# One Fourier row half folded in a new order, small copies moved between engines, and weight loads tied to a later step

## The chip, the cores and the metric

The kernel runs on one core of a Trainium2 chip. A core has a matrix engine (TensorE, in the profile PE; its weight loads are the row PEld), a vector engine (VectorE, DVE), an activation engine (ScalarE, ACT), a general engine (GpSimd, POOL) and a sync engine (SP) that here only issues transfers. Each engine works through its own list of instructions strictly in order. Transfers issued by POOL go into one queue (q0 in the profile), those issued by SP into another (q1), and both are carried by the same 16 DMA engines. The metric is the time of the program on the device in microseconds (us); lower is better.

## What is computed

The reference has two parts. The first is chunked attention over 4 batches of 8 heads, 768 rows and 64 columns: each chunk of 32 rows looks at 8 memory keys and at the rows from 16 before to 8 after it. The second takes the attention output x (4 x 768 x 512) and mixes it:

```python
X = np.fft.fft(x, axis=1)
X = np.fft.fft(X, axis=2)
mixed = np.real(X).astype(np.float32)
u = x + mixed
mu = np.mean(u, axis=-1, keepdims=True)
var = np.mean((u - mu) ** 2, axis=-1, keepdims=True)
un = (u - mu) / np.sqrt(var + 1e-06)
ch = np.maximum(un @ w_ch1, 0.0) @ w_ch2
return (u + ch).astype(np.float32)
```

## The kernel before

The heads are taken in 16 pairs, four to a batch (`HP` = 4). A pair n goes through `attention(n)` (L867): its q and k are loaded by POOL, its v by SP; q and k are transposed on PE and copied out of the transpose bank (`e_qT`, `e_kT`); the memory keys are copied into the key tile (`e_mkT`, L404); then come scores, exponentials on ACT, the products with v on PE, and a normalisation on DVE (`e_norm`) that writes the pair's columns of `xsb`. The 768 rows stand as six tiles of 128 rows; "half g" means three of them, and `t_norm[n, g]` is the task that finishes half g of pair n.

A batch whose four pairs are done is Fourier transformed. For batch 0 this is `first_fourier` (L997), which works in half rows so that it can begin before the last pair is done. It uses symmetry: with `par` 0 and 1 (even and odd columns of the result) and `ab` 0 and 1 (cosine and sine part), four folded tiles of 128 columns are made from the 512 columns of x. In `before` one fold takes three steps on DVE: `g_zy` (L591) adds or subtracts columns 0-127 and 256-383 (the two pairs that are done first); `g_ff(..., last=0)` (L598) adds or subtracts columns 129-255 read backwards, and sets the small column 0 of the fold by a copy or a zero; `g_ff(..., last=1)` adds or subtracts columns 385-511 read backwards, and for (par, ab) = (1, 1) sets column 0 by a subtraction. Columns 128-255 belong to the pair done third (n = 2) and columns 384-511 to the one done last (n = 3), so only the last step waits for the last pair.

After a fold ACT rounds it to 16 bits (`g_hi`, L627), DVE makes the rest that rounding left (`g_lo`, L631), and PE multiplies both with tables of cosines and sines (`g_rows`, L656): 12 matmuls for each of the eight (half, par, ab), besides two groups of one-row matmuls (`g_row`, L644) for the middle column, which POOL prepares (`g_mid`, L636). Then the row result is split again (`e_up` on ACT, `e_rest` and `e_dn` on DVE), the column transform is done on PE (`e_columns`, L669, tile `pm`), the sum, mean and variance on DVE, the centred rows on ACT (`e_un`), their transposes on PE and copies on DVE (`e_unT`). Only then can the two matrix products of batch 0 run: `e_ch1` (L734, tile `ph`) with the first weights, `e_ch2` (tile `pc`) with the second. From there on PE is to be kept full with these products, which are marked as fillers, while attention and Fourier steps of the later batches go on beside them.

What runs when is decided in Python before anything is emitted. `Plan` (L37) holds tasks with an engine, an assumed cost, the tasks they come after, and the buffers that they take and give. It goes through an imagined time and gives each free engine the first task, by rank, that is ready; the rank is the order of creation where none is given. The chosen order is then fixed on each engine. So an assumed cost that changes can change the order everywhere. Where PE has nothing ready before the first fold is done, dummy matmuls are placed (`e_fill`, L825, tile `idle`). `behind=t` holds a task back until task t has been placed; it adds no wait on the chip, but puts the instruction later into its engine's list.

POOL's list around the change is: the q and k loads of pairs 4 and 5, `g_mid(0)`, four loads of the first weights `w1` (L988, 512 KB each as stored, cast from 32 to 16 bits), `g_mid(1)` among them, the loads of pair 6, four loads of the second weights `w2` (L993), the loads of pair 7 and so on. The q and k loads use three buffers each, those of v four. Loads of pair 6 are placed behind the last `w1` load, and `w2` behind the loads of pair 6 (`t_ck`). The `w1` loads are placed behind `t_norm[3, 1]`. A list `t_mark` collects the task of the last fold step of (par, ab, half) = (0, 0, 1); nothing uses it in `before`.

## Time and profile before

| | |
|---|---|
| median of 7 runs | 287.92 us (286.25 to 293.1) |
| the profiled execution | 286.05 us, its span 284.3 us |
| granted TensorE clock, mean | 0.998 |
| PE, DVE, ACT, POOL busy | 268.1, 166.0, 158.9, 58.0 us |
| PE busy from 65.4 to 218.0 us | 151.98 of 152.60 us |

The span is the time from the first to the last instruction; 1.75 us of the profiled execution lie outside it. PE counts as busy with dummy matmuls too, and matmuls overlap, so a busy PE says that it was fed, not that it did needed work. A row of the timeline gives start, length, engine, line, operation, the tiles written and read, and in brackets how long the engine had waited and for what.

### The profile page before, as it was taken

To read this page: it belongs to the slowest core of one execution; us is meant where nothing else is said; L and a number is where in the kernel's file an instruction comes from. 1 tells how busy PE (TensorE), PEld (TensorE's weight loads), DVE (VectorE), ACT (ScalarE), POOL (GpSimd) and SP (SyncE) were. 2 spreads that over 40 slices of the span, in tenths; PEclk is the share of its full clock that TensorE was granted. 3 is DMA by queue.
4 is the path that set the end of the run, shared out by engine and by line. 5 is a ranking of instruction groups with operands and counts; after the bars stand their busy time and mean duration, and the time that the engine had idled before them with its cause. 6 is when DMAs were issued, how large, how long until landed. Compare 5 with 4: busy or idle time off the path is not lost.

```text
span 284.3 us, 7145 instructions
## 1 busy us (share of the span) xinstructions
PE 268.1 (94%) x2943; PEld 171.0 (60%) x2943; DVE 166.0 (58%) x359; ACT 158.9 (56%) x286; POOL 58.0 (20%) x106
## 2 busy tenths in 40 slices
PE   0599998999999999999999999999999999999994
PEld 0466797766575666755756655556754645545644
DVE  7968998972077953899874990887396012012012
ACT  6887448597755578447735468047634722712700
POOL 8844643231210272621010020101002000000000
PEclk9999999999999999999999999999999999999999
DMA  6999999999999999999986462397024434004204
GB/s 106 201 179 159 192 203 201 198 196 191 185 213 237 137 221 177 169 174 212 218 112 155 125 138 48 114 148 220 2 41 107 113 73 112 2 37 111 39 37 111
DMA packets 116112, 39.92 MB, mean 140 GB/s; under 512 B 104560, under 2 KB 111472, under 8 KB 116080
## 3 DMA queue, kind: packets, MB, share of 16 engines
q1 hardware_dynamic: 93888, 23.54, 45.5%
q0 software_dynamic: 21472, 15.21, 33.4%
q10 hardware_dynamic: 720, 0.72, 0.8%
q8 instruction: 23, 0.38, 0.5%
q14 instruction: 9, 0.07, 0.1%
HBM read 37.36 MB, written 13.37 MB: 178 GB/s over the span
## 4 chain that ended last, share of the span: by engine, by line
PE 77%; DMA 13%; POOL 6%; issue 1%; DVE 1%; ACT 0%; POOLq 0%; DVEq 0%
PE pc L752 29%; PE ph L737 28%; DMA qs<-in_q_dram 9%; PE ps L527 5%; DMA w_sb<-in_moe_w_ch_dram 4%; PE xa L455 4%; PE xo L455 3%; PE pm L677 3%; PE sc L431 2%; PE idle L828 1%; PE trq L375 1%; DMA out_dram<-osb 1%; PE trk L375 1%; PE pm L578 1%; POOL qs L347 1%
## 5 line engine op out<-in xcount | busy, mean ns | idle before, releaser
L737 PE MATMUL ph<-unT,w_sb 128*128 128x384 f16 x512 | 88.5, 326 | 0.6 <-ACT hT L745 0.6
L745 ACT ACTIVATE hT<-ph 128x384 f16<-128x384 f32 x128 | 62.0, 493 | 47.2 <-PE ph L737 45.8
L752 PE MATMUL pc<-w_sb,hT 128*128 128x512 f16 x368 | 83.8, 379 | 0.0
L737 PEld LDWEIGHTS <-w_sb 128*128 128x128 f16 x512 | 48.5, 98 | 32.8 <-issue 1.8
L752 PEld LDWEIGHTS <-hT 128*128 128x128 f16 x368 | 34.8, 98 | 39.3 <-issue 0.4
L777 DVE SCALAR_TENSOR_TENSOR osb<-pc,rstd,xsb 128x512 f32<-128x512 f32 x23 | 17.3, 750 | 60.3 <-PE pc L752 58.8
L439 ACT ACTIVATE e<-sc,mbias 128x384 f32<-128x384 f32 x64 | 33.6, 578 | 11.1 <-PE sc L431 10.9
L697 ACT ACTIVATE un<-xsb,mu_s 128x512 f16<-128x512 f32 x24 | 17.1, 722 | 19.2 <-DVE mu_s L692 19.2
L691 DVE BATCH_NORM_STATS2 st<-xsb 128x6 f32<-128x512 f32 x24 | 16.6, 692 | 0.7
L539 ACT CAST up<-ps 128x386 f16<-128x386 f32 x16 | 9.7, 604 | 11.9 <-PE ps L527 10.5
L512 ACT CAST hi<-ff 128x768 f16<-128x768 f32 x12 | 9.9, 830 | 9.8 <-DVE ff L504 9.8
L455 PEld LDWEIGHTS xa<-va,e 128*64 128x64 f32 x384 | 12.6, 138 | 4.4 <-issue 3.4
L455 PE MATMUL xa<-va,e 128*64 128x65 f32 x384 | 14.9, 227 | 0.0
L544 DVE TENSOR_TENSOR up<-ps,up 128x386 f16<-128x386 f32 x16 | 9.6, 597 | 8.5 <-ACT up L539 8.5
L455 PE MATMUL xo<-va,e 128*64 128x65 f32 x384 | 14.1, 223 | 0.0
L431 PE MATMUL sc<-qT,kTb 64*128 64x64 bf16 x384 | 11.5, 194 | 2.7 <-ACT e L439 1.9
L431 PEld LDWEIGHTS <-kTb 64*128 64x128 bf16 x384 | 8.0, 96 | 10.1 <-issue 7.1
L517 DVE TENSOR_TENSOR lo<-ff,hi 128x768 f16<-128x768 f32 x12 | 11.3, 952 | 4.5 <-ACT hi L512 4.4
L683 DVE TENSOR_TENSOR xsb<-pm,xsb 128x512 f32<-128x512 f32 x15 | 10.1, 675 | 4.8 <-PE pm L677 4.7
L465 DVE RECIPROCAL zs<-xa 128x6 f32<-128x6 f32 x16 | 3.0, 188 | 17.0 <-PE xa L455 16.9
L455 PEld LDWEIGHTS xo<-va,e 128*64 128x64 f32 x384 | 12.6, 138 | 0.4 <-ACT e L439 0.3
L487 DVE TENSOR_TENSOR zy<-xsb 128x768 f32<-128x768 f32 x12 | 11.4, 954 | 0.1
(149 smaller groups left out, 357.4 us busy)
## 6 DMA issues: line engine op xcount, KB each, us to landing
va<-in_v_dram SPq DMA_DIRECT2D x32, 220.0 KB
w_sb<-in_moe_w_ch_dram POOLq DMA_DIRECT2D x8, 512.0 KB, 15.0
out_dram<-osb SPq DMA_DIRECT2D x12, 256.0 KB
qs<-in_q_dram POOLq DMA_DIRECT2D x12, 192.0 KB, 6.4
ks<-in_k_dram POOLq DMA_DIRECT2D x12, 192.0 KB, 6.7
x_rows<-xsb POOLq DMA_DIRECT2D x3, 768.0 KB, 5.3
xr<-x_back POOLq DMA_DIRECT2D x3, 768.0 KB, 5.3
out_rows<-osb SPq DMA_DIRECT2D x9, 256.0 KB
```

The source lines that it names most:

```text
L431: nc.tensor.matmul(sc[:, hh, t6, :], kT[r0:r0 + 64, t, :], qT[r0:r0 + 64, ts(t, 64)], start=True, stop=True, tile_position=(r0, 0))
L439: nc.scalar.activation(e1[:, :, :, ts(half, 32)], sc[:, :, 0:6, ts(half, 32)], AFT.Exp, bias=mbias[:, half:half + 1], scale=1.0 / math.sqr ...
L455: nc.tensor.matmul(xa[64 * half:64 * half + 64, st, hh, 0:65], e1[:, hh, t6, :], v1[:, hh, 6 * g + t6, 0:65], start=True, stop=True)
L487: nc.vector.tensor_tensor(zy_of[b, par][:, :, c0:c0 + P], xb[:, :, c0:c0 + P], xb[:, :, HD + c0:HD + c0 + P], ALU.add if par == 0 else ALU ...
L517: nc.vector.tensor_tensor(lo[:, ab].rearrange(fl), ff_of[b, par][:, ab].rearrange(fl), hi[:, ab].rearrange(fl), ALU.subtract)
L527: nc.tensor.matmul(out_[:, sp, :], part[:, ab, sp * 3 + st, c0:c1], tab[:, sp, st, :], start=(st == 0 and i == 0), stop=(st == 2 and i == 1))
L691: nc.vector.bn_stats(st6, xs[b][:, kt, :])
L697: nc.scalar.activation(un, xs[b][:, kt, :], AFT.Identity, bias=mu_of[b][:, kt, 0:1], scale=-1.0)
L737: nc.tensor.matmul(ph[:, 0:384], w1_sb[:, dt, ts(ht, P)], unT_of[b][:, dt, sh * 384:(sh + 1) * 384], start=(dt == 0), stop=(dt == NDT - 1))
L745: nc.scalar.activation(hT_of[b, sh][:, ht, :], ph[:, 0:384], AFT.Relu, bias=0.0, scale=-1.0)
L752: nc.tensor.matmul(pc_of[b, sh, stl], hT_of[b, sh][:, ht, ts(stl, P)], w2_sb[:, ht, :], start=(ht == 0), stop=(ht == NHT - 1))
L777: nc.vector.scalar_tensor_tensor(osb, pc, rstd_of[b][:, st:st + 1], xs[b][:, st, :], ALU.mult, ALU.add)
```

## The change

In half 1 of the first Fourier transform, columns 128-255 and 384-511 (of the pairs n = 2 and n = 3) are now first added or subtracted in reading order (`g_w`, twice, once for each par), into the unused half of the `zy` tile. The fold is then one step from two sums (`g_both`, four times), where it had been two steps (eight times). Half 0 keeps its two steps. The small column 0 of each fold becomes an instruction of its own (`g_col`): seven of the eight are done on ACT and one, (1, 1) of half 0, on POOL at rank 20.1, just behind `g_mid(0)`. `g_hi` waits for its column as well. The memory keys of pair 4 (n == `HP`) are copied by ACT in place of DVE. Assumed costs change: 0.5 for the first fold steps that had 0.62, 0.25 for the memory keys that had 0.2. The `w1` loads are placed behind the fold of (0, 0, 1), now a `g_both`, and no longer behind the last normalisation.

```diff
--- before.py
+++ after.py
@@ -403,7 +403,7 @@
 
     def e_mkT(n):
         b, pr = seq[n]
-        nc.vector.tensor_copy(
+        (nc.scalar.copy if n == HP else nc.vector.tensor_copy)(
             kTb[n % NKT][:, :, MEM0:MEM0 + NMEM],
             mkT[:, b * HP + pr, :].unsqueeze(1).to_broadcast([P, NT, NMEM]))
 
@@ -603,16 +603,34 @@
         plus = ab == par
         if last:
             plus = plus == (par == 0)
-        if not last:
-            if ab == 0:
-                nc.vector.tensor_copy(ff[:, :, 0], zy[:, :, 0])
-            elif par == 0:
-                nc.vector.memset(ff[:, :, 0:1], 0.0)
-        elif (par, ab) == (1, 1):
-            nc.vector.tensor_tensor(ff[:, :, 0], xb[:, :, P], xb[:, :, HD + P], ALU.subtract)
         nc.vector.tensor_tensor(ff[:, :, 1:P], (ff if last else zy)[:, :, 1:P],
                                 rev_ap(xb, 2 * P - 1 + HD * last, P - 1, [[DM, 3]]),
                                 ALU.add if plus else ALU.subtract)
+
+    def g_w(par):
+        xb, sl = xs[0][:, 3:6], slice(0, 3)
+        nc.vector.tensor_tensor(zy_of[0, par][:, sl], xb[:, :, P:2 * P], xb[:, :, HD + P:HD + 2 * P],
+                                ALU.add if par == 0 else ALU.subtract)
+
+    def g_col(par, ab, g):
+        zy = zy_of[0, par]
+        ff = ff_of[0, par][:, ab, 3 * g:3 * g + 3]
+        if ab == 0:
+            nc.scalar.copy(ff[:, :, 0], zy[:, 3 * g:3 * g + 3, 0])
+        elif par == 0:
+            nc.scalar.copy(ff[:, :, 0], zero[:, 0:1].to_broadcast([P, 3]))
+        elif g == 1:
+            nc.scalar.copy(ff[:, :, 0], zy[:, 0:3, 0])
+        else:
+            xb = xs[0][:, 0:3]
+            nc.gpsimd.tensor_tensor(ff[:, :, 0], xb[:, :, P], xb[:, :, HD + P], ALU.subtract)
+
+    def g_both(par, ab):
+        zy = zy_of[0, par]
+        ff = ff_of[0, par][:, ab, 3:6]
+        nc.vector.tensor_tensor(ff[:, :, 1:P], zy[:, 3:6, 1:P],
+                                rev_ap(zy, P - 1, P - 1, [[P, 3]]),
+                                ALU.add if ab == par else ALU.subtract)
 
     def g_hl(par, which):
         if (par, 0) not in g_of:
@@ -882,7 +900,7 @@
                 nc.gpsimd.tensor_copy(gate[64:65], va[n % NV][64:65, 1, NT - 1, 0:1])
 
             t_gate = add("POOL", 0.1, e_gate, [lv])
-        mk = t_mk[n] = add("DVE", 0.2, lambda: e_mkT(n), [t_mkT, t_kTz[n % NKT], t_mk.get(n - 1)],
+        mk = t_mk[n] = add("ACT" if n == HP else "DVE", 0.25, lambda: e_mkT(n), [t_mkT, t_kTz[n % NKT], t_mk.get(n - 1)],
                            take=("kTb",), behind=t_norm.get((HP - 1, 1)) if n in (HP, HP + 1) else None)
         if b >= TURNED:
             eq = add("SP", 1.2, lambda: e_flip_q(n), [lq], take=("qT",), give=("qs",),
@@ -987,7 +1005,7 @@
         if n == HP + 1:
             t_w1.extend(add("POOL", 0.7, lambda dt=dt: nc.gpsimd.dma_start(
                 w1_sb[:, dt, :], moe_w_ch1[ts(dt, P), :]), moved=2.4, grain=0.32, late=2.0,
-                behind=t_norm[HP - 1, 1], rank=t_ck[n]["rank"] + 0.1) for dt in range(NDT))
+                behind=t_mark[0], rank=t_ck[n]["rank"] + 0.1) for dt in range(NDT))
             t_ck[n] = t_w1[-1]
         else:
             t_w2.extend(add("POOL", 0.7, lambda g=g: nc.gpsimd.dma_start(
@@ -1001,25 +1019,45 @@
                 zy = add("DVE", 0.5, lambda par=par, g=g: g_zy(par, g),
                          [t_norm[0, g], t_norm[1, g], t_sines],
                          take=("unT",) if g == 0 else ())
+                if g == 1:
+                    w_ = add("DVE", 0.52, lambda par=par: g_w(par), [zy, t_norm[3, 1], pre[par, 1, 0]])
+                    for ab in range(2):
+                        col = add("ACT", 0.25, lambda par=par, ab=ab: g_col(par, ab, 1),
+                                  [w_ if par else zy, pre[par, ab, 0]])
+                        pre[par, ab, 1] = [w_, zy, col]
+                    continue
                 for ab in range(2):
-                    pre[par, ab, g] = add("DVE", (0.62 if ab == 0 else 0.5),
+                    pre[par, ab, g] = add("DVE", 0.5,
                                           lambda par=par, ab=ab, g=g: g_ff(par, ab, g, 0),
                                           [zy, t_norm[2, g]],
                                           take=("fold",) if (ab, g) == (0, 0) else (),
                                           give=("unT",) if (ab, g) == (1, 1) else ())
             t_mid[g] = add("POOL", 0.9, lambda g=g: g_mid(g), [t_norm[2, g], t_norm[3, g]],
                            rank=20)
+            if g == 0:
+                for par in range(2):
+                    for ab in range(2):
+                        pool = (par, ab) == (1, 1)
+                        pre[par, ab, 2] = add("POOL" if pool else "ACT", 0.4 if pool else 0.25,
+                                              lambda par=par, ab=ab: g_col(par, ab, 0),
+                                              [pre[par, 0, 0], t_norm[3, 0] if pool else None],
+                                              rank=20.1 if pool else None)
             t_row[g] = add("PE", 1.2, lambda g=g: g_row(g), [t_mid[g], t_neg, t_row.get(0), t_dz],
                            take=("acc",) if g == 0 else ())
             for par in range(2):
                 for ab in range(2):
                     end = (ab, g) == (1, 1)
-                    ff = add("DVE", 0.5 + 0.1 * par * ab,
-                             lambda par=par, ab=ab, g=g: g_ff(par, ab, g, 1),
-                             [pre[par, ab, g], t_norm[3, g]])
+                    if g == 0:
+                        ff = add("DVE", 0.5,
+                                 lambda par=par, ab=ab, g=g: g_ff(par, ab, g, 1),
+                                 [pre[par, ab, g], t_norm[3, g]])
+                    else:
+                        ff = add("DVE", 0.55, lambda par=par, ab=ab: g_both(par, ab),
+                                 pre[par, ab, 1][:2], give=("unT",) if ab == 1 else ())
                     if (par, ab, g) == (0, 0, 1):
                         t_mark.append(ff)
-                    hi = add("ACT", 0.5, lambda par=par, ab=ab, g=g: g_hi(par, ab, g), [ff],
+                    hi = add("ACT", 0.5, lambda par=par, ab=ab, g=g: g_hi(par, ab, g),
+                             [ff] + (pre[par, ab, 1][2:] if g == 1 else [pre[par, ab, 2]]),
                              take=(("hl",), ("hT",))[par] if (ab, g) == (0, 0) else ())
                     lo = add("DVE", 0.48, lambda par=par, ab=ab, g=g: g_lo(par, ab, g), [hi],
                              give=("fold",) if end else ())
```

## The prediction

> **What bounds the kernel now.** I read the page first, for the share of PE and the forty slices.
>
> ```profile
> span 284.3 us, 7145 instructions
> PE 268.1 (94%) x2943; PEld 171.0 (60%) x2943; DVE 166.0 (58%) x359; ACT 158.9 (56%) x286; POOL 58.0 (20%) x106
> PE   0599998999999999999999999999999999999994
> DMA  6999999999999999999986462397024434004204
> ```
>
> PE is fed for 94% of the span, and the transfer engines are full to the twentieth slice, some 142 us. So time can be won only where PE is unfed or fed with dummies. The stretches of PE, asked for one by one, show where:
>
> ```profile
> 16.00:34.40 18.40, 17.65 (x411) 13.47 (x411) 15.02 (x37) 13.20 (x22) 8.24 (x17) 1.00 1.05 173
> 34.40:43.90 9.50, 9.50 (x112) 8.94 (x110) 9.04 (x26) 4.85 (x9) 5.22 (x8) 1.00 1.14 204
> 43.90:55.70 11.80, 10.55 (x206) 9.00 (x205) 10.35 (x23) 7.73 (x14) 3.18 (x5) 1.00 1.18 198
> 55.70:65.40 9.70, 9.60 (x141) 6.29 (x136) 6.41 (x18) 8.87 (x18) 2.26 (x3) 1.00 1.22 198
> 65.40:218.00 152.60, 151.98 (x1649) 95.01 (x1650) 103.18 (x200) 88.64 (x162) 24.29 (x32) 1.00 0.91 153
> ```
>
> The columns are the stretch, then busy time and count of PE, PEld, DVE, ACT and POOL, the granted clock, the DMA share and GB/s. From 65.4 us on PE loses 0.6 us in 152.6: what the front saves, the end gets, unless a new hole opens. In the first stretch dummies are part of PE's time: 25 of them lie between 21.5 and 34.4 us at about 0.19 us each, 4.7 us. The third stretch is 1.25 us short. The timeline tells why the row transform begins only at 34.4 us and where the 1.25 us lie:
>
> ```profile
> 30.93 0.55 DVE L613 TENSOR_TENSOR ff<-ff,xsb 128x381 f32<-128x381 f32 x1
> 31.96 0.80 ACT L393 COPY qT<-trq 128x768 bf16<-128x768 bf16 x1 [1.94 <-PE trq L375]
> 32.66 0.93 ACT L629 CAST hi<-ff 128x384 f16<-128x384 f32 x2
> 33.20 1.03 DVE L633 TENSOR_TENSOR lo<-ff,hi 128x384 f16<-128x384 f32 x2
> 37.64 1.48 DVE L613 TENSOR_TENSOR ff<-ff,xsb 128x381 f32<-128x381 f32 x3
> 45.55 0.35 PE L431 MATMUL sc<-qT,kTb 64*128 64x64 bf16 x12 [0.85 <-ACT e L439]
> ```
>
> The first fold of half 0 is ready at 31.5 us, but ACT first waits 1.94 us for the queries of pair 4 and copies them, and rounds the fold only at 32.66. And 0.85 of the 1.25 us is PE waiting for the exponential of pair 4. Last, the transfers, in the timeline, the keys' and weights' landing times, and the DMA view from 36 to 44 us:
>
> ```profile
> 31.75 1.15 POOL L988 DMA_DIRECT2D w_sb<-in_moe_w_ch_dram  x2
> 45.65 0.65 POOL L347 DMA_DIRECT2D qs<-in_q_dram  x1 [2.17 <-DMA w_sb<-in_moe_w_ch_dram]
> 65.44 0.40 PEld L375 LDWEIGHTS <-qs 96*64 96x64 bf16 x16 [0.27 <-DMA qs<-in_q_dram]
> q0 software_dynamic: 427, 1.57, 98.7%
> q1 hardware_dynamic: 329, 0.08, 8.7%
> ```
>
> The first weights are issued from 31.75 to 34.8 us and the last lands 13.0 us after its issue, at 47.8; the first product with them begins at 55.70. Pair 6's queries, issued at 35.33, land 13.7 us later at 49.0 and are used at 54.14. Pair 7's (45.65) land at 65.4, where PE waits 0.27 us for them. While weights flow, q1 (values) moves 0.08 MB against 1.57.
>
> **The change part by part.** The sum is made against the profiled execution, 286.05 us, which lies 1.87 us under the median of 287.92; I carry the difference over to the median.
>
> *VectorE's saving.* The eight fold passes of half 1 start about 0.50 us apart (1.48 us for three). They become two sums as wide as `zy` (1.02 us for two) and four passes: 8 x 0.50 against 2 x 0.52 + 4 x 0.50, a saving of 0.96 us. The small columns last 0.16 to 0.18 us each but delay the next instruction by only 0.07 to 0.12 (the copy at 26.92 and the pass at 27.04): four copies, two subtractions and two zeros give 0.5. The keys' copy gives 0.1. Together 1.6 us of DVE between 26 and 41 us.
>
> *What of it reaches PE.* PE has no hole from 34.4 to 43.9 us: eight groups of 12 matmuls at 1.02 us and one of `g_row` at 1.0 fill it. A DVE that is 1.6 us quicker there gains nothing by itself; PE covers it, and the saving would count only from the point at which PE were the faster. The gain must come from an earlier start. Of the removed columns 0.2 us lie before 30 us, so the first fold is ready near 31.3. If ACT then rounds it ahead of the query copy of pair 4 (whose input is ready only at 31.96), the rest is ready near 32.6 in place of 33.7. PE still owes the one-row matmuls, which end at 33.5, so the rows begin near 33.4: 1.0 us sooner. The ends are 0 (the order on ACT stays) and 1.2 us (32.66 less 31.45). I take 1.0, because the copy waits for a transfer there and the fold does not; 0.2 of it goes back because the key transposes of pair 4 (0.36 us), now ahead of the rows, fall among them. So 0.8.
>
> *Memory keys of pair 4 on ACT.* On DVE they are copied at 40.99 us, and the key copy (42.44, 1.04 us), scores (43.89) and exponential queue behind. ACT is busy 4.85 of 9.50 us in that stretch, and pair 4's transposed keys are there from 34.1. With the copy on ACT (ACT's smallest row is 0.20 us, its 128x768 copy 0.80; I take 0.27) the chain can start some 6 us sooner, so the wait of 0.85 us should go, and PE has work while the last row results are split. Ends: 0 (the pair of exponentials makes PE wait elsewhere) and 1.25 us (the whole hole). I take 0.85. What is late next is the tail of the transform, sum, variance, rows and transposes, from 45.8 to 55.7.
>
> *Columns on ACT and POOL.* Seven copies by the 0.20 us row are 1.4 us, in a stretch where ACT is idle half the time; if ACT were the bound they would cost all of that. The one on POOL is one subtraction like the `mid` one, 0.24 to 0.37 us; behind it are `mid(1)`, needed by PE near 37 us, and the weight loads, which now come later anyway. Cost nothing, up to 1.4 us without the cover. [...]
>
> *Weights behind a fold.* This adds no wait but sends w1 from POOL some 4 us later: the first `g_both` comes where DVE has done half 0, some 36 us, so w1 is issued from about 36 to 38.3, the loads of pair 6 from 38.3 in place of 35.33, w2 from 39.6 in place of 36.61, pair 7 after that. The earlier q0 load lands at 34.6 us (27.75 + 6.9), so q0 runs dry for up to 4 us. The engines are not idle: the values on q1 take them. All of q0 behind is then about 4 us late, and the values early. w1 lands near 52 (first use 55.7, or 54 if the front gains): slack 2 us. Pair 6 lands near 53, used at 54.1: slack about 1. Pair 7 lands near 69.4 where it is used at 65.4: late, but 7 of 16 groups of `ph` not yet run by 65.4 (0.65 us each, 4.6 us) and the first `pc` groups are there to fill PE. A gain isn't seen in it; a loss has its ends at 0 and 4 us. I take 0.1, nearest to the slack of w1 and pair 6. [...]
>
> Sum: 0.8 + 0.85 - 0.1 = 1.55, and 0.3 for later holes between 46 and 56 us of the 0.4 left: 1.85 us. 286.05 - 1.85 = 284.2 in the profiled execution's terms, 286.07 by the median; I say 286.0.
>
> **The rivals.**
> *Nothing reaches the end.* The ACT order stays and the 0.85 us wait moves to another exponential: 0.2 to 0.5 us gained, 287.5. For it: DVE and PE are both full from 34 to 44 us, and each engine's order is fixed ahead.
> *More is won.* All of 1.25 us, rows 1.2 us sooner, and the 0.1 us and 0.6 us holes later closed: 3.2 us, 284.7. For it: 4.7 us of dummies are there to be replaced. Against: the one-row matmuls and the key loads.
> *Slower: the second batch's rows come too late for the first's products.* Pair 7 ends batch 1; its queries 4 us late put batch 1's transform up to 4 us late, while PE eats batch 0's products 2 us earlier. PE now ends those at 126.6 us, fills 1.5 us with values, and begins batch 1's at 128.16; the third turned row block it needs has been sent by 123.7 (five in 6.46 us from 119.84), and its flight is not shown, so the slack is 0 to 4.5 us; I take 2.2. Against a shift of 4 + 2 that is a hole of 3.8 us, less 1.85 gained: 288.0, by the median 289.9. It decides once the delay that reaches batch 1's rows is over 2 us. Against it: between pair 7's queries and batch 1's transform lie slacks; the first rest of that transform is done on DVE at 89.5 us (0.95 from 88.56), and PE takes it up only at 96.8.
>
> **How the numbers follow.** Chances: forecast 0.42 (own range 285.0 to 287.0), more won 0.13, nothing 0.25, slower 0.20. What a measurement of this kernel can tell from no change is about 0.5%, 1.4 us. Most of the forecast (0.36) and all of "more" lie below 286.5: faster 0.49; 0.06 of it, "nothing" and a bit of "slower" within: 0.31; slower 0.20. The range takes in "more" and much of "slower": 284.0 to 289.6.
>
> **What would show it.** Right: ACT rounds the first fold ahead of pair 4's query copy, rows from 33.4 us, fewer than 25 dummies, no 0.85 us wait on an exponential near 45, the first `ph` near 54, w1 landing near 52. Wrong: PE waiting for w1 or pair 6's loads between 52 and 60 us, a PE hole before batch 1's first `ph` near 126, or rows still starting at 34.4.

## The result, and the profile after

The changed kernel takes 284.28 us (median of 25 runs, 283.28 to 287.28). The kernel before, run beside it, takes 286.92 us (median of 65 runs, 285.56 to 294.12). The ratio is 0.992 with a 95% interval of 0.990 to 0.994: 2.3 us faster, between 1.7 and 2.8. The profiled executions are closer together: 286.05 us before and 284.9 us after, spans 284.3 and 283.2 us. So the profiles below show 1.1 us of the 2.3. Each ratio, here and below, leaves out the executions in a kernel's slower state, and a median does not, so a median can lie higher than its ratio says.

From the page of the changed kernel, the span, the busy times, and the slices of PE:

```profile
span 283.2 us, 7142 instructions
PE 267.3 (94%) x2941; PEld 170.6 (60%) x2941; DVE 164.1 (58%) x348; ACT 158.7 (56%) x294; POOL 58.7 (21%) x107
PE   0599999999999999989999999999999999999995
```

And the same five stretches of PE as in the prediction (stretch, then busy time and count of PE, PEld, DVE, ACT and POOL, granted clock, DMA share, GB/s):

```profile
16.00:34.40 18.40, 18.04 (x416) 14.14 (x416) 15.25 (x35) 14.39 (x29) 7.68 (x17) 1.00 1.07 178
34.40:43.90 9.50, 9.50 (x127) 8.64 (x125) 7.62 (x18) 6.57 (x15) 5.55 (x9) 1.00 1.06 200
43.90:55.70 11.80, 11.15 (x226) 9.65 (x226) 11.00 (x28) 6.44 (x11) 2.55 (x4) 1.00 1.17 197
55.70:65.40 9.70, 9.70 (x91) 6.12 (x86) 5.07 (x13) 8.49 (x17) 3.56 (x4) 1.00 1.22 197
65.40:218.00 152.60, 151.07 (x1666) 94.28 (x1664) 101.46 (x195) 86.46 (x160) 24.12 (x30) 1.00 0.90 151
```

The third stretch is now 0.65 us short where it was 1.25 us. VectorE's busy time from 16 to 43.9 us fell from 24.06 to 22.87 us. The last stretch, which had lost 0.6 us, now loses 1.53 us. One new hole is all of it. It lies in the slice of PE's row that shows an 8, the eighteenth of forty (120.4 to 127.4 us).

The timeline of the changed kernel around the first fold, and then the first matmul of the row transform in the kernel before:

```profile
29.96 0.28 ACT L406 COPY kTb<-mkT 128x96 bf16<-128x96 bf16 x1
30.54 0.56 DVE L606 TENSOR_TENSOR ff<-ff,xsb 128x381 f32<-128x381 f32 x1
31.18 0.51 ACT L647 CAST hi<-ff 128x384 f16<-128x384 f32 x1 [0.94 <-DVE ff L606]
31.60 0.79 ACT L393 COPY qT<-trq 128x768 bf16<-128x768 bf16 x1
33.33 0.54 PE L375 MATMUL trk<-turn_b,ks 100*64 100x100 bf16 x16
33.80 0.26 PE L684 MATMUL ps<-cosS,hi 128*128 128x193 f16 x1
39.15 0.35 PE L431 MATMUL sc<-qT,kTb 64*128 64x64 bf16 x12
```

```profile
34.52 0.25 PE L666 MATMUL ps<-cosS,hi 128*128 128x193 f16 x1
```

ScalarE now rounds the first fold (31.18) ahead of the query copy of pair 4 (31.60). The row transform begins at 33.80 us in place of 34.52 (the prediction read 34.4), 0.72 us sooner. Some 0.4 us of that can be chance: in pad1 below, whose lists are the same, it begins at 34.24. The memory keys of pair 4 are copied at 29.96 us, 11 us sooner than before, and that pair's scores come at 39.15, in the middle of the row transform. The wait of 0.85 us on the exponential near 45 us is gone.

The timeline of the changed kernel at the weight loads on POOL:

```profile
33.43 2.21 POOL L1006 DMA_DIRECT2D w_sb<-in_moe_w_ch_dram  x4
35.61 0.68 POOL L347 DMA_DIRECT2D qs<-in_q_dram  x1
```

All four `w1` loads go out together from 33.43 us, straight behind `mid(1)`, and pair 6's queries at 35.61. Before, two of the loads went at 31.75, two at 34.23, and the queries at 35.33. The last load lands 12.7 us after its issue, at 47.8 us, exactly where it did. Nothing is 4 us later.

At last the new hole, in PE's and SP's timelines of the changed kernel (SPq: SP's queue of issues; `unT<-un` is a transposed row block of batch 1, `kU<-ks` the turned keys of pair 12):

```profile
117.31 1.23 SPq L727 DMA_TRANSPOSE unT<-un  x1
118.64 1.34 SPq L384 DMA_TRANSPOSE kU<-ks  x1
120.07 6.09 SPq L727 DMA_TRANSPOSE unT<-un  x4
122.98 1.90 PE L770 MATMUL pc<-w_sb,hT 128*128 128x512 f16 x8
127.97 2.27 PE L755 MATMUL ph<-unT,w_sb 128*128 128x384 f16 x13 [1.53 <-DMA unT<-un]
```

Batch 0's products end at 124.9 us (126.6 before) and the values that follow at 126.4. PE is 1.7 us earlier there. Then batch 1's first product waits 1.53 us for a row block and starts at 127.97, where it started at 128.16 with no wait. The first product needs row blocks 0, 3 and 4, which SP sends first, third and fourth. So nearly all that the front had won is lost at this point in the profiled execution; the 1.1 us at the end come from behind it (the wait of 0.58 us for `hT` at 166.11 us in the kernel before is gone, for one).

### The profile page after: what moved, and what is told of

It reads as the page before. It is cut to its first block, busy times and chain, and to the rows that moved or that the text cites. A ratio compares the mean times of both kernels' runs of the same rounds, so it can differ in the third digit from the quotient of the medians.

```text
span 283.2 us, 7142 instructions
## 1 busy us (share of the span) xinstructions
PE 267.3 (94%) x2941; PEld 170.6 (60%) x2941; DVE 164.1 (58%) x348; ACT 158.7 (56%) x294; POOL 58.7 (21%) x107
## 3 DMA queue, kind: packets, MB, share of 16 engines
q0 software_dynamic: 21472, 15.21, 33.4%
## 4 chain that ended last, share of the span: by engine, by line
PE 88%; POOL 4%; DVE 3%; DMA 2%; ACT 1%; issue 1%; SPq 0%; POOLq 0%
PE ph L755 30%; PE pc L770 27%; PE ps L527 6%; PE xa L455 4%; PE xo L455 4%; PE pm L695 4%; PE ps L684 3%; PE sc L431 3%; PE idle L846 2%; DMA unT<-un 2%; PE trk L375 2%; PE trq L375 1%; PE pc L776 1%; DVE xsb L701 1%; DVE st L709 1%
## 5 line engine op out<-in xcount | busy, mean ns | idle before, releaser
L755 PE MATMUL ph<-unT,w_sb 128*128 128x384 f16 x512 | 86.7, 326 | 1.5 <-DMA unT<-un 1.5
L763 ACT ACTIVATE hT<-ph 128x384 f16<-128x384 f32 x128 | 61.1, 492 | 47.6 <-PE ph L755 46.1
L770 PE MATMUL pc<-w_sb,hT 128*128 128x512 f16 x368 | 85.4, 380 | 0.0
L755 PEld LDWEIGHTS <-w_sb 128*128 128x128 f16 x512 | 49.2, 98 | 33.9 <-issue 2.0
L770 PEld LDWEIGHTS <-hT 128*128 128x128 f16 x368 | 34.1, 98 | 37.9 <-issue 0.7
L570 POOL DMA_DIRECT2D xr<-x_back x3 | 2.3, 768 | 51.1 <-DMA x_back<-x_rows 51.1
L393 ACT COPY qT<-trq 128x768 bf16<-128x768 bf16 x12 | 9.5, 793 | 6.0 <-PE trq L375 6.0
L347 POOL DMA_DIRECT2D qs<-in_q_dram x12 | 8.0, 669 | 20.3 <-PE xa L455 13.2
```

Of the source, the lines that this page charges most:

```text
L755: nc.tensor.matmul(ph[:, 0:384], w1_sb[:, dt, ts(ht, P)], unT_of[b][:, dt, sh * 384:(sh + 1) * 384], start=(dt == 0), stop=(dt == NDT - 1))
L763: nc.scalar.activation(hT_of[b, sh][:, ht, :], ph[:, 0:384], AFT.Relu, bias=0.0, scale=-1.0)
L770: nc.tensor.matmul(pc_of[b, sh, stl], hT_of[b, sh][:, ht, ts(stl, P)], w2_sb[:, ht, :], start=(ht == 0), stop=(ht == NHT - 1))
```

## The experiments

All twelve were timed against the kernel before, in five rounds. The columns are: ratio with its interval, over many executions; and, from the one profiled execution of each, the first-product matmuls (`ph`) done by PE between 50 and 70 us, a rough measure of how far the front has got (in the timeline of the changed kernel eight of them start at 60.60 us and the next group at 61.90, so 0.163 us each); the hole before batch 1's first product near 126 us; and the wait of the column transform of batch 2 near 158 us (`pm` on `xsb`, L587).

| kernel | ratio | `ph` at 50-70 us | hole near 126 | wait near 158 |
|---|---|---|---|---|
| before | 1 | 52 | 0 | 0 |
| after | 0.992 (0.990-0.994) | 64 | 1.5 | 0 |
| cols_dve | 0.987 (0.982-0.991) | 64 | 0 | 0 |
| rows_first | 0.992 (0.987-0.996) | 64 | 0 | 0.2 |
| pad1 | 0.992 (0.988-0.996) | 64 | 0 | 0 |
| query_first | 0.992 (0.989-0.995) | 64 | 0 | 0 |
| keys_rows_first | 0.996 (0.992-1.000) | 59 | 0 | 4.1 |
| before_keys | 1.001 (0.997-1.004) | 60 | 0 | 1.7 |
| weights_back | 1.001 (0.996-1.006) | 57 | 0 | 2.2 |
| costs_only | 1.002 (0.998-1.006) | 52 | 3.2 | 0 |
| before_weights | 1.008 (1.004-1.013) | 53 | 3.8 | 0 |
| flips | 1.013 (1.008-1.018) | 64 | 5.1 | 0 |
| keys_dve | 1.022 (1.018-1.027) | 56 | 6.0 | 0 |
| keys_dve_hold | 1.029 (1.024-1.035) | 58 | 7.7 | 0 |

The table is the main finding, but its three last columns sort the kernels only roughly. With 64 `ph`, no hole of 3 us and no wait of 1.7 us the ratio is 0.987 to 0.992; with a wait of 1.7 to 2.2 us near 158 it is 1.001; with a hole of 3.8 us or more it is 1.008 to 1.029. Within these groups they order nothing: the changed kernel has a hole of 1.5 us that pad1 has not, and the same ratio. And one profiled execution need not stand for the rest. Of the twelve executions of costs_only, six had a mean granted clock of 0.997 or more and took 285.87 to 287.83 us; six had 0.994 or less and took 289.60 to 294.40 us. The profiled one, with the hole of 3.2 us, is of the second kind (290.07 us). In keys_rows_first, too, it is one of the longest (290.84 us, against a median of 286.05).

### Is VectorE's saving worth anything? (pad1, cols_dve, query_first)

pad1 does each of the two new wide sums twice, 1.0 us more on VectorE with every list otherwise as in the changed kernel.

```diff
-        nc.vector.tensor_tensor(zy_of[0, par][:, sl], xb[:, :, P:2 * P], ...
+        for _ in range(2):
+            nc.vector.tensor_tensor(zy_of[0, par][:, sl], xb[:, :, P:2 * P], ...
```

> The two new sums of half 1 are each done twice on VectorE (same values), so VectorE has 1.0 us more work between 34 and 36 us; the order on every engine is that of the changed kernel. Theory (PE covers VectorE's saving from 34 to 44 us): 0 to 0.4 us over the changed kernel, ratio to before 0.992 to 0.9935. Rival (VectorE is the bound there and its saving is the gain): 1.0 us over, ratio 0.9955 or more.

It takes 284.33 us against 284.28. The extra microsecond costs nothing that five rounds can see, although the interval (0.988 to 0.996) just reaches the 0.9955 of the rival. So the saved VectorE time was most likely not what won.

pad1 shows a second thing. Its lists are those of the changed kernel, with the two doubled sums as the only difference, and yet it has no hole near 126 us. SP's and PE's timelines of pad1:

```profile
118.02 1.24 SPq L384 DMA_TRANSPOSE kU<-ks  x1
119.35 5.32 SPq L728 DMA_TRANSPOSE unT<-un  x4
126.81 6.67 PE L756 MATMUL ph<-unT,w_sb 128*128 128x384 f16 x40
```

The keys of pair 12 stand between the first and the second row block as before, and PE waits for nothing. So the hole of 1.53 us belongs to the profiled execution of the changed kernel and not to its lists alone. How many of its 25 executions have it is not on record.

cols_dve puts all eight small columns back on VectorE.

```diff
-            nc.scalar.copy(ff[:, :, 0], zy[:, 3 * g:3 * g + 3, 0])
+            nc.vector.tensor_copy(ff[:, :, 0], zy[:, 3 * g:3 * g + 3, 0])
...
-                        col = add("ACT", 0.25, lambda par=par, ab=ab: g_col(par, ab, 1),
+                        col = add("DVE", 0.1, lambda par=par, ab=ab: g_col(par, ab, 1),
...
-                        pre[par, ab, 2] = add("POOL" if pool else "ACT", 0.4 if pool else 0.25,
+                        pre[par, ab, 2] = add("DVE", 0.1,
```

> The changed kernel with its small columns back on VectorE (half 1's four copies and half 0's share, in the places that the order gives them). My theory: the columns cost VectorE 0.07 to 0.12 us each, 0.5 us together, under a PE that is full from 34 to 44 us; so the front stays: rows from 33.8 to 34.2 us, first product near 56, ratio 0.990 to 0.995 as long as no hole before batch 1's first product is over 2 us. Rival, that the columns' place matters by itself (VectorE is the bound of the front): rows end 0.5 us later or more and the ratio is 0.994 to 0.998. A second rival, from the runs so far: the new assumed durations reorder the list, and a hole of 3 us or more before batch 1's first product decides; then the ratio is 1.000 or above.

It takes 283.44 us, ratio 0.987, the lowest of all and below the 0.990 to 0.995 expected, although its interval (to 0.991) overlaps that of the changed kernel (from 0.990). The timeline of VectorE in cols_dve shows what the columns cost it, and the stretches what PE does from 43.9 us and at 126:

```profile
29.23 0.16 DVE L619 COPY ff<-zy 128x3 f32<-128x3 f32 x1
29.30 0.16 DVE L621 COPY ff<-zero 128x3 f32<-128x3 f32 x1
```

```profile
43.90:55.70 11.80, 11.72 (x243) 10.29 (x243) 11.25 (x27) 7.44 (x13) 3.39 (x6) 1.00 1.17 198
126.00:136.00 10.00, 10.00 (x73) 5.95 (x72) 9.01 (x15) 7.81 (x16) 1.13 (x2) 1.00 1.17 217
```

Two columns start 0.07 us apart. PE is full in both stretches. Moving the columns off VectorE was no part of the gain that is seen. Whether cols_dve is really better than the changed kernel, and through what, stays open: there is no hole at 126 us, but pad1 has none either.

query_first puts the query copy of pair 4 ahead of the first rounding again.

```diff
+            if n == HP:
+                t_hi0[0]["behind"] = eq
...
+                    if (par, ab, g) == (0, 0, 0):
+                        t_hi0.append(hi)
```

> The changed kernel, but on ScalarE the query copy of pair 4 stands ahead of the first rounding of the fold, as before; the rest of the order is kept but for the first rows and a few dummies. Theory (the earlier rounding is half of the gain): the first rows start near 34.3 us again and 0.4 to 0.8 us are lost, ratio 0.9935 to 0.995. Rival (the order on ScalarE is indifferent as PE makes it up): under 0.2 us, ratio 0.992.

The timeline of PE in query_first, up to the first row matmul:

```profile
34.15 0.54 PE L375 MATMUL trk<-turn_b,ks 100*64 100x100 bf16 x16
34.62 0.67 PE L671 MATMUL ps<-cosS,mid 128*1 128x193 f16 x6
35.13 0.66 PE L671 MATMUL ps<-odd,mid 128*1 128x193 f16 x6
35.72 0.26 PE L684 MATMUL ps<-cosS,hi 128*128 128x193 f16 x1
```

The rows begin at 35.72, 1.9 us after those of the changed kernel (34.3 was expected), and the time is 284.84 us, a ratio of 0.992 again (0.989 to 0.995). PE did not stand still: the second group of one-row matmuls, which the changed kernel has at 36.94 and 37.44, was done first. An earlier start of the rows is by itself worth nothing that this measurement sees, as long as PE has something else that must be done anyway.

query_first, too, has pair 12's keys ahead of the second row block and no hole. It sends the fourth row block at 123.51 us, and PE begins with it at 127.19 without a wait, at most 3.7 us later; in the changed kernel the block sent at 122.74 held PE until 127.97, 5.2 us. So the time from issue to use differed by 1.5 us or more, which is more than the 1.34 us of the keys' issue.

### Do the weights' place and the keys' place carry the gain? (weights_back, before_weights, keys_dve, before_keys, costs_only)

weights_back undoes one line of the change.

```diff
-                behind=t_mark[0], rank=t_ck[n]["rank"] + 0.1) for dt in range(NDT))
+                behind=t_norm[HP - 1, 1], rank=t_ck[n]["rank"] + 0.1) for dt in range(NDT))
```

> The changed kernel with the first weights' loads placed behind the last normalisation again. Theory (the move delayed nothing on the chip, as the queue is full of earlier loads until 34.5 us; it only changed what the planned order supposes after 54 us): last first-weight landing within 0.5 us of 47.8, ratio 0.989 to 0.994. Rival (the later weights give values and later pairs room, which is part of the gain): ratio 0.995 or more, PE waits for a load between 50 and 70 us.

That expectation was missed: ratio 1.001 (0.996 to 1.006), the whole gain of some 2.5 us gone. The loads themselves still go out at 33.5 to 35.2 us and the last lands near 48.0 (47.8 in the changed kernel), so it is not the transfers. It is the lists. The timeline of PE in weights_back, and then that of the changed kernel:

```profile
51.35 0.53 PE L375 MATMUL trq<-ident_b,qs 96*64 96x96 bf16 x16
53.30 0.54 PE L375 MATMUL trk<-turn_b,ks 100*64 100x100 bf16 x16
57.21 0.97 PE L755 MATMUL ph<-unT,w_sb 128*128 128x384 f16 x5 [0.23 <-DVE unT L733]
```

```profile
55.44 0.51 PE L375 MATMUL trq<-ident_b,qs 96*64 96x96 bf16 x16
55.89 1.48 PE L755 MATMUL ph<-unT,w_sb 128*128 128x384 f16 x8
57.29 0.55 PE L375 MATMUL trk<-turn_b,ks 100*64 100x100 bf16 x16
```

In weights_back the transposes of pair 6 stand ahead of the first products, which start 1.3 us later; seven fewer are done by 70 us (1.1 us). More is lost near 158 us, as the timeline and one stretch of weights_back show (ten of its twelve executions had a mean clock of 0.994 or less):

```profile
158.45 0.61 PE L695 MATMUL pm<-cosD,up 128*128 128x256 f16 x2 [2.20 <-DVE xsb L587]
157.63 0.69 DVE L585 TENSOR_TENSOR xsb<-pm,xr 128x510 f32<-128x510 f32 x1 [3.38 <-DMA xr<-x_back]
```

```profile
155.00:160.00 5.00, 2.80 (x24) 1.50 (x24) 2.28 (x4) 1.05 (x2) 0.00 (x0) 0.81 0.58 193
```

The sum of batch 2 waits for its mirrored rows (`xr`), which come back through memory, and PE waits 2.20 us behind it; the mean clock of the stretch is 0.81.

before_weights makes only this line's change, on the kernel before.

```diff
-                behind=t_norm[HP - 1, 1], rank=t_ck[n]["rank"] + 0.1) for dt in range(NDT))
+                behind=t_mark[0], rank=t_ck[n]["rank"] + 0.1) for dt in range(NDT))
```

> The kernel before with only the first weights moved behind the fold. The run that put the weights back lost the whole gain, so if the weights' place alone carries it, this gives 0.990 to 0.995, with more than 60 first-product matmuls done between 50 and 70 us against 52 before. If the parts only work together (my theory: the weights' place acts through the order that is fixed ahead, not through the transfers), this is within 0.997 to 1.005, the first weights are issued within 1 us of where they were, near 32 to 33 us, and land within 1 us of 47.8. If the loads really come 4 us later, as my prediction had it, w1 lands near 52 and PE waits for it.

It is slower, 290.43 us (1.008), and its front is where it was (53 against 52). So the line is needed for the gain and does harm alone. The place of the weights does not carry the gain alone. My range of 0.997 to 1.005 was too good as well, since the new lists also opened a hole of 3.8 us near 126 us. The four loads start at 33.98 us and the last lands near 49.0, each a little later than expected, and PE waits for none of them.

keys_dve puts the memory keys of pair 4 back on VectorE; before_keys moves only them, on the kernel before; costs_only changes only the assumed costs, on the kernel before.

```diff
-        (nc.scalar.copy if n == HP else nc.vector.tensor_copy)(
+        nc.vector.tensor_copy(
...
-        mk = t_mk[n] = add("ACT" if n == HP else "DVE", 0.25, ...
+        mk = t_mk[n] = add("DVE", 0.25, ...
```

> The changed kernel, but the memory keys of pair 4 are copied by VectorE again. Theory (early keys give PE work while the row results are split): a wait of PE for an exponential of pair 4 near 45 us is back, 0.5 to 1.0 us lost, ratio 0.994 to 0.9955. Rival (the keys move is indifferent): ratio 0.992, wait or no wait.

```diff
-        nc.vector.tensor_copy(
+        (nc.scalar.copy if n == HP else nc.vector.tensor_copy)(
...
-        mk = t_mk[n] = add("DVE", 0.2, ...
+        mk = t_mk[n] = add("ACT" if n == HP else "DVE", 0.2, ...
```

> The kernel before with only the memory keys of pair 4 on ScalarE. Theory (the early keys are most of the gain): 1 us or more of lead in products done by 70 us, ratio 0.993 to 0.998 unless a hole opens before batch 1's first product, which then has to show in the profile. Rival (the row half's new folds are most of the gain): ratio 0.999 to 1.0 with no lead by 70 us.

```diff
-        mk = t_mk[n] = add("DVE", 0.2, lambda: e_mkT(n), ...
+        mk = t_mk[n] = add("DVE", 0.25, lambda: e_mkT(n), ...
...
-                    pre[par, ab, g] = add("DVE", (0.62 if ab == 0 else 0.5),
+                    pre[par, ab, g] = add("DVE", 0.5,
```

> The kernel before, with only the assumed costs changed (0.5 for the first fold steps that had 0.62, 0.25 for the memory keys): no instruction is other than before, only the order. Theory (the gain is made of an earlier rounding on ScalarE plus early keys): only the first of the two, 0.4 to 0.8 us under before, ratio 0.997 to 0.9985. Rival (the whole gain is a matter of the order that the assumed costs give): 2 us under, ratio 0.993. Rival (VectorE's work is the gain): ratio 1.0.

keys_dve takes 293.68 us (1.022), before_keys 287.16 us (1.001), costs_only 288.71 us (1.002); each lies outside what my theory expected of it. costs_only has the earlier rounding (31.79 us) and the earlier rows (33.85 us), and neither more `ph` than before nor a gain. That is what the rival said for whom VectorE's work is the gain; pad1 speaks against that one. The keys on ScalarE by themselves bring 60 of the 64 `ph` by 70 us, but PE then waits 1.44 us, to 64.8 us, for queries that have not landed, and the lead does not last: batch 1's first product starts at 128.35 us, against 128.16 in the kernel before. A wait of 1.7 us near 158 follows. Taken out of the changed kernel they cost 8 of the `ph` (1.3 us), and then a hole of 6.0 us opens near 126. From SP's and PE's timelines of keys_dve, and its stretches:

```profile
127.26 1.23 SPq L384 DMA_TRANSPOSE kU<-ks  x1
128.58 3.87 SPq L727 DMA_TRANSPOSE unT<-un  x2
133.88 6.44 PE L755 MATMUL ph<-unT,w_sb 128*128 128x384 f16 x22 [6.03 <-DMA unT<-un]
```

```profile
130.00:135.00 5.00, 1.12 (x4) 0.58 (x5) 3.58 (x7) 0.00 (x0) 0.00 (x0) 0.76 0.91 214
135.00:140.00 5.00, 5.00 (x19) 2.35 (x17) 0.00 (x0) 1.96 (x4) 0.00 (x0) 0.56 0.93 239
```

The needed row block is sent behind the turned keys of pair 13 (127.26), and PE comes out of the hole with a clock of 0.56. The hole is 4.5 us longer than in the changed kernel; 1.3 us are lost ahead of it, and by an estimate from the clocks of these two stretches (0.76 and 0.56, or 0.50 from 132.6 to 139.4 us and 1.00 beside it) some 2.8 us by the clock, over about 5.5 us of matmuls: 8.6 of the 8.7 us between the two spans.

### What makes the hole near 126 us? (keys_dve_hold, flips, rows_first, keys_rows_first)

My theory was SP's list: SP issues in the order of its list (in keys_dve the turned keys, at 127.26 for 1.23 us, and only then the next row block, at 128.58), and what stands ahead of the third needed row block holds it up. keys_dve_hold puts the flips of pair 13 behind the fourth row block.

```diff
+            if n == TURNED * HP + 1:
+                eq["behind"] = done[1][0][4]
```

> The kernel with the memory keys of pair 4 on VectorE (the one 2.2% slower than before), and on SyncE the transposing transfers of pair 13 held behind the first four row transposes of batch 1; PE's order is the same up to batch 1's first product. Theory (its time was lost in the 6 us hole before that product, made by a wait that stands ahead of the row transposes in SyncE's list): hole under 2 us, ratio to before 0.995 to 1.003. Rival (copying the keys on VectorE itself costs the time): ratio over 1.015.

The hole did not shrink, it grew to 7.75 us. SP's timeline of keys_dve_hold shows why:

```profile
122.26 3.66 SPq L727 DMA_TRANSPOSE unT<-un  x2
126.02 0.62 SPq L360 DMA_DIRECT2D va<-in_v_dram  x1
129.16 1.31 SPq L365 DMA_DIRECT2D va<-in_mem_v_dram  x1
130.56 3.85 SPq L727 DMA_TRANSPOSE unT<-un  x3
```

The flips of pair 13 left, and the loads of a pair's values moved up into their place, from 126.02 to 130.47. flips gives the row blocks in another order (0, 3, 4, 1, 2, 5) in the changed kernel.

```diff
-                               [un], behind=t_un.get(kts[i - 1]) if i else None,
+                               [un],
...
+        if b > 0:
+            for one, two in ((0, 3), (3, 4), (4, 1), (1, 2), (2, 5)):
+                t_un[two]["behind"] = t_un[one]
```

> The changed kernel, with the row transposes of batches 1 to 3 sent in the order 0, 3, 4, 1, 2, 5 in place of 0, 1, 3, 4, 2, 5: the first half of each second product needs 0, 3 and 4 alone. Theory (the lead of the changed kernel is partly lost waiting for the third needed transpose near 126 us): no PE wait there, 0.2 to 1.0 us under the changed kernel, ratio to before 0.988 to 0.991. Rival (that wait is made good later): ratio 0.992.

It missed too, 290.44 us and a hole of 5.1 us: again the planner let a load of values in, from 121.26 to 125.85, and the second and later row blocks were sent only from 125.95. These two misses spoke for the theory's cause but left it untested, since each time something else took the place. So the last two hold back everything of that kind: the keys of pair 12, what follows them, and the values of pairs 14 and 15, in the changed kernel (rows_first) and in keys_dve (keys_rows_first).

```diff
-                 behind=t_x2.get(b - 2),
+                 behind=done[1][0][4] if n in (14, 15) else t_x2.get(b - 2),
...
-                                 give=("ks",), late=5.0, loose=True, behind=eq)
+                                 give=("ks",), late=5.0, loose=True, behind=done[1][0][4] if n == TURNED * HP else eq)
```

> The changed kernel with the flip of pair 12's keys (issued at 118.64 for 1.34 us between the first and second row block of batch 1) behind the fourth row block, and the values of pairs 14 and 15 behind it as well. My theory: the 1.53 us hole before batch 1's first product is the 1.34 us of that issue on SP, since the third needed row block was normalised at 119.9 and sent only at 122.7; so the hole shrinks to 0.3 us or less, and if what is saved there reaches the end the median is 282.8 to 284.0, ratio 0.986 to 0.991. Rival, that the hole is later work come early and is paid again behind it (pair 12's scores then wait for its keys): the hole goes, a wait near 132 to 140 us takes its place, and the time stays at 284.0 to 285.

> The changed kernel with the memory keys of pair 4 on VectorE (ratio 1.022, a hole of 6.0 us before batch 1's first product) and, as in the run before this one, the flip of pair 12's keys, what follows it and the values of pairs 14 and 15 behind the fourth row block. My theory: nothing that waits for a load stands ahead of the needed row blocks any more, so the hole is under 1.5 us, the clock stays above 0.99 through 130 to 140 us, and what is left of the loss is the 1.5 to 1.8 us that this kernel was behind at 66 to 120 us: 285.5 to 287.0, ratio 0.994 to 1.001. Rival, that the row blocks are made too late by then: the hole stays at 4 us or more and the ratio at 1.012 or above.

SP's timeline of rows_first:

```profile
117.93 5.21 SPq L727 DMA_TRANSPOSE unT<-un  x4
123.24 1.23 SPq L384 DMA_TRANSPOSE kU<-ks  x1
```

Four row blocks go out in one run. Batch 1's first product starts at 125.5 and waits for no row block. In keys_rows_first the hole is gone as well (first product at 127.1, clock 1.00 from 130 to 140 us), and the median falls from 293.68 to 286.05 us, inside the 285.5 to 287.0 expected. That is the clean case: all six executions of keys_dve had a mean clock of 0.988 or less, ten of the twelve of keys_rows_first 0.998 or more, and 7.6 of 9.4 us come back by taking a few issues out of the way. The hole of 6 us was the list's.

In rows_first it is different. The time is 284.70 us (0.992), not the 282.8 to 284.0 of my theory: here the rival was nearer, although the interval (0.987 to 0.996) still holds a gain of 1 us. pad1 gives the likely reason: with the changed kernel's order and no hole it takes 284.33 us, so the order of rows_first had little to win. That the order made the hole of 1.53 us is not shown. A little is also waited for later. DVE in rows_first and then in the changed kernel, at batch 2's sum:

```profile
160.06 0.69 DVE L585 TENSOR_TENSOR xsb<-pm,xr 128x510 f32<-128x510 f32 x1 [1.34 <-DMA xr<-x_back]
```

```profile
159.79 0.69 DVE L585 TENSOR_TENSOR xsb<-pm,xr 128x510 f32<-128x510 f32 x1 [0.27 <-DMA xr<-x_back]
```

The mirrored rows arrive at about 160 us in both (their last transfer is issued at 153.04 and 153.01 us). VectorE waits 1.34 us for them in place of 0.27, and PE 0.17 us. So near 158 us stands the next limit. The profiled execution of keys_rows_first is one of its longest (290.84 us), so its wait of 4.1 us at that place shows where it can be lost and not how much is lost as a rule.

## Why the prediction was right, and where not

The sign was right, and so was the size of the change: 1.85 us forecast, 2.3 us (1.7 to 2.8) measured, and 1.1 us between the two profiled executions. The time named, 286.0 us, was too long: 284.28 lies under the forecast's own range of 285.0 to 287.0, though within the wide range of 284.0 to 289.6. Of these 1.7 us, 1.0 is the time before, 287.92 from 7 runs and 286.92 from 65.

The way there was partly another one, and the sum agrees partly by luck. 0.8 of its 1.85 us is a term of which query_first and costs_only show nothing, and undoing the weights' place, which stands in the sum as a loss of 0.1 us, costs some 2.5 us.

Of the signs named, the rounding ahead of the query copy, the lost wait near 45 us and fewer dummies came (23 with 4.78 us, against 25 with 5.00 us, which the prediction added up to 4.7). Rows from 33.4 us, the first `ph` near 54 and `w1` landing near 52 did not. And the hole before batch 1's first `ph`, named as a sign of being wrong, stood in the profiled execution.

**"VectorE's saving" gains nothing by itself.** Right. 1.6 us were forecast, 1.2 us are seen up to 43.9 us (1.9 us over the whole span, 166.0 against 164.1), and giving 1.0 us back (pad1) costs nothing that is seen.

**"What of it reaches PE", 0.8 us.** The order on ScalarE came as forecast, but the rows begin at 33.80 and not 33.4, since PE does the key transposes of pair 4 (33.33) ahead of them and not among them: 0.72 us sooner and not 1.0. More than that, the term is wrong as a price. In query_first the rows start 1.9 us later than that and the ratio is the same 0.992; in costs_only they start at 33.85 and nothing is gained. PE filled the time with work that it owed anyway. The prediction had seen that PE is full from 34.4 us, and still priced an earlier start of one kind of its work as a gain.

**"Memory keys of pair 4 on ACT", 0.85 us, and 0.3 us for later holes.** The wait near 45 us went, as forecast, and in the third stretch PE won 0.6 us. But keys_dve, with the keys back on VectorE, has no wait there either (PE busy for 11.11 of 11.80 us), so the keys' place was not needed to remove it. As a price the term was near: without this part the changed kernel does 8 fewer `ph` by 70 us, 1.3 us against 0.85 + 0.3 (all 12 more are 12 x 0.163 = 2.0 us). What it left out is the hole of 6.0 us that then opens near 126.

**"Columns on ACT and POOL" cost nothing.** Right, and they gain nothing (cols_dve, 0.987).

**"Weights behind a fold", -0.1 us.** Wrong in mechanism. It said in one breath that this adds no wait and that `w1` is sent 4 us later. On the chip the loads follow `mid(1)` at once, from 33.43 us, and the last lands at 47.8 us as before; pair 6's queries go out at 35.61 in place of 35.33 and land at 49.1 in place of 49.0. The part acts only through the lists that the planner makes from its imagined times: without it the kernel is at 1.001, and alone it is at 1.008. The prediction named what could be late and did not ask what else the planner would put in another order.

**The first `ph` near 54 us** did not come: 55.9, against 55.7. It is the number of them by 70 us that changed.

**The rival "slower".** Its place was right (batch 1's first product, near 126 us) and its mechanism half: PE came 1.7 us earlier to row blocks that were not there yet. It put the lateness on pair 7's queries and took a price of 3.8 us; in the profiled execution of the changed kernel it is 1.5 us, in pad1, with the same lists, nothing. It also took the third block sent for the third one needed, which is the fourth sent, from 123.77 us in the kernel before and not by 123.7. In four of the twelve experiments, those with a hole of 3.8 us or more, the largest loss in the profile is here.

## What to carry to other kernels

Where lists are fixed ahead by a planner, an edit acts twice: at its own place, and through every list that comes out differently. Here three parts taken one at a time gave 1.001, 1.002 and 1.008, all together 0.992 (the new fold alone was not run), and large parts of the difference lay 90 to 125 us behind the edit; so undo one part at a time and look at the whole span, not only at the edited stage. An engine that only issues transfers can hold up the busiest one, as SP did here (7.6 of 9.4 us came back in keys_rows_first by taking a few issues out of the way): look in its own timeline at what stands ahead of the transfer that the busiest engine waits for. An earlier start of one piece of work was worth nothing where the engine had other owed work to put in its place (query_first, rows 1.9 us later at the same ratio of 0.992). And one profiled execution can hold a hole that another with the same lists has not: before a hole is explained by the order of a list, look whether it comes back.

## What the runs showed of the hardware

A hole can cost more than its length. After the 1.53 us hole of the changed kernel the granted clock stays at 1.00 (128 to 138 us). The stretches of costs_only around its hole of 3.19 us:

```profile
128.00:130.00 2.00, 0.10 (x4) 0.00 (x0) 1.93 (x4) 0.00 (x0) 0.46 (x1) 1.00 0.62 81
132.00:134.00 2.00, 2.00 (x9) 0.89 (x7) 2.00 (x6) 0.98 (x2) 0.00 (x0) 0.56 1.07 338
134.00:136.00 2.00, 2.00 (x19) 0.97 (x18) 0.10 (x1) 1.54 (x3) 0.00 (x0) 0.59 0.87 165
136.00:138.00 2.00, 2.00 (x24) 1.13 (x22) 0.37 (x2) 1.64 (x4) 0.00 (x0) 1.00 0.74 167
```

PE is back at work from 131.29 us, but at a clock of 0.56 to 0.59 until about 136 us, which loses some 1.7 us more (0.42 of 4 us). Such spells came after the other holes of 3.8 us and more near 126 us too. In before_weights (3.8 us) the clock is 0.81, 0.50 and 0.83 in the three stretches of 2 us from 130 to 136 us. The stretches from 130 to 135 and from 135 to 140 us have 0.59 and 0.73 in flips (5.1 us), 0.76 and 0.56 in keys_dve (6.0 us), and 0.64 and 0.68 in keys_dve_hold (7.7 us). If these means are made of time at 0.50 and time at 1.00, an estimate from them (the clock that is missing times the stretch, over 0.50) gives 3.4 us at 0.50 in costs_only and before_weights, and 6.8 us, twice as long, in the other three.

A shorter hole had such a spell as well. In weights_back, after a hole of only 2.20 us, the clock is 0.81 from 155 to 160 us and 0.85 from 160 to 165 us, again 3.4 us at 0.50 by the same estimate, and two `pm` matmuls take 0.61 us at 158.45, where two at 161.97 take 0.38. After 1.53 us (the changed kernel) and 1.73 us (before_keys, where two `pm` matmuls right behind the hole take 0.39 us) there is no drop. What sets a spell off, and why some are twice as long, no run shows.

A transposing transfer took SP 1.23 to 1.34 us to issue in the rows shown here that hold one alone, and the row block that ended the hole of the changed kernel let PE go on 5.2 us after the start of its issue (122.74 to 127.97 us). Ahead of the row blocks in SP's list the turned keys took 1.23 us (127.26 us in keys_dve) and 1.34 us (118.64 us in the changed kernel), and the loads of one pair's values 4.5 us (126.02 to 130.47 us in keys_dve_hold).
